# Two first feed-forward blocks built by quarters, first loads cut anew, and the joined score step's half query block read in one run

## The chip, the cores and the metric

The kernel runs on one NeuronCore of one Trainium2 chip. The metric is device time in microseconds (us) of one execution; the figure of a kernel is the median of its runs. The core's engines are TensorE (PE in the profile, with its weight loads as PEld), VectorE (DVE), ScalarE (ACT), GpSimd (POOL) and SyncE (SP). Transfers are issued by SP, ACT and POOL and carried by 16 DMA engines. POOL's transfers (queue q0) convert float32 in memory to bfloat16 on the way; those of SP and ACT (q1, q10) don't convert.

## The reference

Attention with a decay bias, then a gated feed-forward part over its output. Cut to what matters:

```python
# q, k, v: (8 batches, 8 heads, 576, 64);  s: (8, 8, 576)
scores = 0.125 * q @ k^T
cum    = cumsum(max(s, 0))
scores = where(causal, -1e9, scores + min(-(cum_i - cum_j), 0))
attn   = softmax(scores) @ v
x      = attn as (4608 tokens, 512)
xn     = x / sqrt(mean(x * x) + 1e-6) * rms_g
out    = (silu(xn @ w_gate) * (xn @ w_val)) @ w_out     # 512 -> 1536 -> 512
```

## The kernel before

**Attention.** Each batch has 4 head pairs and 5 key blocks (four of 128 rows, one of 64). K and Q of a batch are loaded, cast to bfloat16 and turned so that the head dimension lies on the partitions. A score step then has keys on the partitions and up to 256 queries (the key block's own and the next) in the free dimension; what lies further off is negligible by the decay, which a check at the end confirms, with a slow general path behind it. ACT takes the exponential, POOL masks, and the attention step multiplies with V (line 437 for the key block behind, 443 for the own one). DVE divides by the row sums, ACT or DVE sums the squares, POOL makes the scale `al_all`, DVE applies it (`x_scale`, L484), and `xs_sb` is turned into `xnT` (columns are tokens), by PE for batch 0 (`xt_step`, L504, copied out at L511).

From batch 3 on, both head groups' scores of one key block are made in one `s_run` (L339 on). Its last run of a batch joins key blocks 3 and 4: for each head pair it makes three matmuls for each half of the rows, one of 128 queries and two of the 64 tail queries (`tail`, L358), against keys 3 and keys 4. The results stand in the order r, p (query 4p + r) that the turned Q blocks have; the tail's queries stand in plain order, so `tail` is read with a step of four.

**Feed-forward.** `ffn(c)` takes 512 tokens at a time, 9 chunks. For each of 12 blocks of 128 hidden units there are four matmuls of 128x512 for the gate (`Gp`, L946), ACT's tanh (L949), four for the value (`Vp`, L955), and two DVE operations (U at L958, Ht at L951), then 4 x 12 matmuls with `wout_sb` (L972). `Gp` and `Vp` take turns in the four banks of `psF`.

**What sets the order.** The instruction order on every engine is written out by hand. Between groups of feed-forward matmuls, `step()` raises `slot[0]` by one (36 slots in a chunk) and lets at most one score step, attention step or turning step of a later batch in, by rules on slots (`can_s`, `can_av`, `can_t`); side queues (`v_side`, `pool_side`, `act_side`, `dve_side`) hold loads and casts with the slot from which they may go. Batch 0 is written out before the chunks begin: its scores, its attention, then four times `x_scale` and `do_xt`, with matmuls into nothing (`warm`, L849, and `stir`) between them. Batch 1's K and Q are loaded by SP in four transfers (`load_kq`: K heads 0 to 3, Q heads 0 to 3, K heads 4 to 7, Q heads 4 to 7) into `kq32`, cast into `kqn`, and turned in the first slots of chunk 0 (L203).

**Weights.** `load_w(src, dst, f0, f1)` lets POOL load blocks f0 to f1 (128 hidden units each, 64 KB a block as it lands) of the gate or the value matrix. Before, in POOL's order: gate 0 to 4, value 0 to 6, gate 4 to 6, and inside chunk 0 gate 6 to 12 (held back by a one-element memset of DVE in `wg_sb`, L1206), value 6 to 9 and 9 to 12, then the two tails of K and Q, V of batch 1 and `wout_sb`.

Of the kernel before, what the change touches and what calls it, by code (L numbers as in the profile page):

```python
# [26 lines left out]
def kernel(  # L27
# [12 lines left out]
    nc = tc.nc  # L40
# [298 lines left out]
    def s_run(b, kb):  # L339
# [13 lines left out]
        for g in (1, 0):  # L353
            for j in (0, 1):
                hp = 2 * g + j
                parts = [(kb, kqTx[:, p, 1, kb:kb + 2, hp, :], 0, 256)]
                if join:
                    tail = kqTx[:, p, 1, 4, hp, 0:64].rearrange("d (p r) -> d r p", r=4)  # L358
                    parts = [(3, kqTx[:, p, 1, 3, hp, :].rearrange("d (r p) -> d r p", r=4), 0, 32),
                             (3, tail, 32, 16), (4, tail, 48, 16)]  # L360
                for i, (c, qT, o, n) in enumerate(parts):
                    for par in (0, 1):
                        rs = slice(par * 64, par * 64 + 64)
                        to = banks[g][par][:, j * 256:j * 256 + 256]
                        if join:
                            to = to.rearrange("k (r p) -> k r p", r=4)[:, :, o:o + n]
                        nc.tensor.matmul(to, lhsT=keys(rs, c, hp), rhs=qT[rs],  # L367
                                         start=(j == 0 and i == 0), stop=(j == 1 and i == len(parts) - 1))
# [159 lines left out]
    K2 = 33  # L528
    slot = [0]
# [254 lines left out]
    def can_s():  # L784
# [9 lines left out]
        if b == 1 and (phase() < 24 and phase() % 2 == 0 or kb == 4 and at("AV", 1, 3, 1) > slot[0]):  # L794
            return False
# [13 lines left out]
    def can_av(clear=False):  # L809
# [5 lines left out]
        if b >= MB and last["XS"] == slot[0]:  # L815
            return False
# [119 lines left out]
    def ffn(c):  # L936

        x0 = (c * DM) % RING
        first[0], chunk[0] = slot[0], c
        Ht = mp.tile([128, FB, DM], BF16, name="Ht", tag="Ht", bufs=2)  # L940
        pend = None
        for fb in range(FB):
            fs = slice(fb * 128, (fb + 1) * 128)
            Gp = psF()
            for cc in range(CC):
                nc.tensor.matmul(Gp, lhsT=wg_sb[:, cc, fs], rhs=xnT[:, cc, x0:x0 + DM],  # L946
                                 start=(cc == 0), stop=(cc == CC - 1))
# [4 lines left out]
            step(tanh=True)  # L952
            Vp = psF()
            for cc in range(CC):
                nc.tensor.matmul(Vp, lhsT=wv_sb[:, cc, fs], rhs=xnT[:, cc, x0:x0 + DM],  # L955
                                 start=(cc == 0), stop=(cc == CC - 1))
# [4 lines left out]
            if fb < FB - 1:  # L961
                step()
# [17 lines left out]
        for tb in range(4):  # L980
            store(tb, [(0, 384), (384, 512)] if c == NCH - 1 and tb == 3 else [(0, DM)])

# [83 lines left out]
    with tc.manual_schedule():  # L1066
# [47 lines left out]

        def stir(n):
# [65 lines left out]
        for g in (0, 1):  # L1181
            for w in (0, 1):
                nc.vector.memset(kq32[0:1, w, 4 * g, 0:1], 0.0)
        for g in (0, 1):
            for w in (0, 1):
                load_kq(nc.sync, 1, w, 4 * g, 4 * g + 4)
# [22 lines left out]

# [6 lines left out]

        def load2(eng, w):
# [4 lines left out]
        def put(queue, n, *fns):  # L1222
            queue.extend((lambda: slot[0] >= n, f) for f in fns)
        put(act_side, 2, lambda: (piece1(ACT, 0, 0, 0, 4), done_cast(0, 0)))
        put(act_side, 6, lambda: piece1(ACT, 0, 1, 0, 2))
        put(pool_side, 2, lambda: fold_v(POOL, 4))
        put(pool_side, 4, lambda: (piece1(POOL, 1, 0, 0, 4), done_cast(1, 0)))
        put(pool_side, 6, lambda: (piece1(POOL, 0, 1, 2, 4), done_cast(0, 1)))
# [12 lines left out]

        check(0, (0,))
# [202 lines left out]
```

## Time and profile before

| | |
|---|---|
| median of 3 runs | 356.08 us (355.93 to 356.49) |
| the profiled execution | 355.58 us, of which the span from first to last instruction is 354.1 us |
| PE busy | 340.6 us, 96% of the span |
| DVE, ACT, POOL busy | 276.9, 213.4, 204.5 us |
| TensorE clock granted | 0.999 of full speed |
| moved by DMA | 45.68 MB, mean 129 GB/s |

Busy time of PE counts a matmul from its start to a modelled end, and matmuls overlap, so it tells less than the distance from one start to the next, which the timeline gives. A row of the timeline is: start, length, engine, line, operation, tiles, count of merged instructions, and in brackets the idle time ahead of it with what ended it. A row of the DMA view gives, for a group of transfers, the issuing queue, count, size of one, and the time from issue to landing. A row of the windows view gives busy time and count of instructions of each engine in a stretch, the granted clock, the busy share of the DMA engines (over 1 where packets overlap) and GB/s.

### The profile page before, as it was taken

What the parts mean: (1) busy time and instruction counts of PE and PEld (TensorE: products, weight loads), DVE (VectorE), ACT (ScalarE), POOL (GpSimd) and SP (SyncE); (2) the same over time, 40 slices, a digit from 0 to 9 for tenths busy, and PEclk for the clock granted to TensorE, in tenths of its full rate; (3) what the DMA queues carried; (4) which work ended last, traced back from release to release, by engine and by line L of the source; (5) the groups of instructions that cost most, each with busy time, mean ns of one, the idle gap of its engine ahead of it and who ended that gap; (6) DMA issues with size and microseconds to landing.
All of it is one profiled execution on the core that took longest, in us unless ns stands there. A gap on an engine that the chain in (4) does not pass through costs nothing.

```text
span 354.1 us, 6889 instructions
## 1 busy us (share of the span) xinstructions
PE 340.6 (96%) x2374; PEld 165.3 (47%) x2419; DVE 276.9 (78%) x524; ACT 213.4 (60%) x471; POOL 204.5 (58%) x337
## 2 busy tenths in 40 slices
PE   5989999999999999999999999999999999999995
PEld 2445444544444444444554454444544554444443
DVE  6697989598967887798889887988798659836840
ACT  3988885878786546855677557654565445224321
POOL 6969754456769986687597987597745310000000
PEclk9999999999999999999999999999999999999999
DMA  7999999999969998999899999495510121020002
GB/s 220 142 213 270 180 175 259 181 211 181 98 123 177 146 179 118 233 141 202 143 170 105 117 131 185 46 113 90 143 29 17 57 94 23 0 91 30 0 34 93
DMA packets 130528, 45.68 MB, mean 129 GB/s; under 512 B 110548, under 2 KB 125656, under 8 KB 130488
## 3 DMA queue, kind: packets, MB, share of 16 engines
q0 software_dynamic: 67056, 13.70, 50.5%
q1 hardware_dynamic: 53792, 24.20, 33.3%
q10 hardware_dynamic: 9640, 7.29, 8.2%
q8 instruction: 20, 0.33, 0.4%
q14 instruction: 20, 0.16, 0.2%
HBM read 37.90 MB, written 9.44 MB: 134 GB/s over the span
## 4 chain that ended last, share of the span: by engine, by line
PE 77%; DVE 8%; POOL 4%; issue 4%; DMA 3%; ACT 2%; SPq 0%; DVEq 0%; POOLq 0%; ACTq 0%
PE psF L972 25%; PE psF L955 21%; PE psF L946 20%; DVE U L958 2%; PE psAV L443 2%; DMA kq<-in_q_dram 2%; DMA kqT<-kqn 2%; PE psS L286 2%; DVE Ht L951 1%; PE psAV L437 1%; DVE x_sb L453 1%; PE psF L367 1%; POOL v_sb L409 1%; POOL v_sb L194 1%; PE psS L367 1%
## 5 line engine op out<-in xcount | busy, mean ns | idle before, releaser
L955 PE MATMUL psF<-xnT,wv_sb 128*128 128x512 bf16 x424 | 109.9, 379 | 0.4
L946 PE MATMUL psF<-xnT,wg_sb 128*128 128x512 bf16 x414 | 109.0, 379 | 1.3 <-ACT xnT L511 0.3
L949 ACT ACTIVATE T<-psF 128x512 f32<-128x512 f32 x108 | 64.6, 598 | 62.9 <-PE psF L946 58.8
L972 PE MATMUL psF<-wout_sb,Ht 128*128 128x512 bf16 (+2 forms) x428 | 98.9, 373 | 1.4 <-issue 0.8
L958 DVE SCALAR_TENSOR_TENSOR U<-T,psF 128x512 bf16<-128x512 f32 x108 | 73.7, 682 | 24.1 <-ACT T L949 23.9
L951 DVE TENSOR_TENSOR Ht<-U,psF 128x512 bf16<-128x512 bf16 x99 | 67.8, 685 | 6.9
L972 PEld LDWEIGHTS <-Ht 128*128 128x128 bf16 x444 | 40.1, 98 | 43.5 <-issue 1.4
L955 PEld LDWEIGHTS <-wv_sb 128*128 128x128 bf16 x432 | 39.6, 98 | 44.5 <-issue 2.9
L946 PEld LDWEIGHTS <-wg_sb 128*128 128x128 bf16 x432 | 39.4, 98 | 42.9 <-issue 2.4
L976 ACT ACTIVATE osb<-psF 128x512 f32<-128x512 f32 (+2 forms) x37 | 21.7, 587 | 58.4 <-PE psF L972 50.8
L384 POOL TENSOR_SCALAR_AFFINE_SELECT E<-E 128x512 bf16<-128x512 bf16 (+1 forms) x50 | 34.8, 704 | 28.5 <-ACT E L380 18.7
L194 POOL DMA_DIRECT2D v_sb<-in_v_dram x40 | 35.3, 885 | 0.2 <-issue 0.2
L484 DVE SCALAR_TENSOR_TENSOR xs_sb<-x_sb,al_all,g_row 128x512 bf16<-128x512 bf16 (+1 forms) x36 | 29.6, 823 | 4.1 <-POOL al_all L477 3.9
L474 POOL TENSOR_SCALAR al_all<-ss_all 128x1 f32<-128x1 f32 (+2 forms) x39 | 11.5, 295 | 35.9 <-ACT xs_sb L461 27.9
L310 ACT ACTIVATE E<-psS,biasK 128x256 bf16<-128x256 f32 (+3 forms) x88 | 29.2, 426 | 2.6 <-PE psS L286 2.6
L453 DVE TENSOR_TENSOR x_sb<-psAV,rZ 128x256 bf16<-128x256 f32 (+1 forms) x66 | 28.0, 424 | 2.3
L522 DVE TENSOR_TENSOR acc<-acc,mag 128x1280 bf16<-128x1280 bf16 x32 | 27.3, 873 | 0.2
L477 POOL TENSOR_TENSOR al_all<-al_all,mhalf 128x1 f32<-128x1 f32 (+2 forms) x39 | 25.2, 645 | 3.2
L443 PEld LDWEIGHTS <-E 128*128 128x128 bf16 x320 | 21.7, 97 | 10.5 <-POOL E L384 0.7
L461 ACT ACTIVATE xs_sb<-x_sb 128x512 bf16<-128x512 bf16 (+1 forms) x37 | 23.3, 629 | 4.6 <-DVE x_sb L453 4.0
L409 POOL TENSOR_TENSOR v_sb<-v_sb,vwx 128x512 bf16<-128x512 bf16 x25 | 25.9, 1037 | 0.1
L443 PE MATMUL psAV<-v_sb,E 128*128 128x65 bf16 x264 | 23.8, 193 | 0.1
(136 smaller groups left out, 379.8 us busy)
## 6 DMA issues: line engine op xcount, KB each, us to landing
out_dram<-osb SPq DMA_DIRECT2D x35, 256.0 KB, 2.7
kq<-in_q_dram ACTq DMA_DIRECT2D x5, 1024.0 KB, 7.5
v_sb<-in_v_dram POOLq DMA_DIRECT2D x32, 128.0 KB, 4.9
kqn<-in_k_dram POOLq DMA_DIRECT2D x20, 128.0 KB, 5.1
kq<-in_k_dram SPq DMA_DIRECT2D x4, 512.0 KB, 5.8
kq<-in_q_dram SPq DMA_DIRECT2D x4, 512.0 KB, 7.5
wout_sb<-in_moe_w_out_dram POOLq DMA_DIRECT2D x2, 768.0 KB, 10.5
kq<-in_q_dram POOLq DMA_DIRECT2D x1, 1024.0 KB, 11.0
```

The source lines that it names most:

```text
L194: nc.gpsimd.dma_start(out=v_sb[0:n, b % 2, c, :, 0:64], in_=v[b, :, c * 128:c * 128 + n, :].rearrange("h p d -> p h d"))
L384: nc.gpsimd.affine_select(out=Ev, in_=Ev, pattern=[[0, 4], [1, nq]], compare_op=ALU.is_ge, fill=0.0, base=0, channel_multiplier=-1)
L409: nc.gpsimd.tensor_tensor(out=v_sb[:, b % 2, c, :, 0:64], in0=v_sb[:, b % 2, c, :, 0:64], in1=vwx[:, c, i:i + H].unsqueeze(2).to_broadcast ...
L443: nc.tensor.matmul(o, lhsT=d, rhs=v_sb[:, p, qb, h, :], start=(j == 0 and qb == 0), stop=(j == 3))
L453: nc.vector.tensor_tensor(out=xo[:, g * 256:(g + 1) * 256].rearrange("p (h d) -> p h d", h=4), in0=pv[R, :, 0:64], in1=rZ[R].unsqueeze(2). ...
L484: nc.vector.scalar_tensor_tensor(out=xs_sb[R, (b * NSC + qb) % NX, :], in0=x_sb[R, (b * NSC + qb) % NX, :], scalar=al_all[R, col:col + 1], ...
L946: nc.tensor.matmul(Gp, lhsT=wg_sb[:, cc, fs], rhs=xnT[:, cc, x0:x0 + DM], start=(cc == 0), stop=(cc == CC - 1))
L949: nc.scalar.activation(out=T, in_=Gp, func=AF.Tanh, scale=0.5)
L951: nc.vector.tensor_tensor(out=Ht[:, fb - 1, :], in0=pend[0], in1=pend[1], op=ALU.mult)
L955: nc.tensor.matmul(Vp, lhsT=wv_sb[:, cc, fs], rhs=xnT[:, cc, x0:x0 + DM], start=(cc == 0), stop=(cc == CC - 1))
L958: nc.vector.scalar_tensor_tensor(out=U, in0=T, scalar=1.0, in1=Gp, op0=ALU.add, op1=ALU.mult)
L972: nc.tensor.matmul(Op[:, p0:p1], lhsT=Ht[:, fb, tb * 128:(tb + 1) * 128], rhs=wout_sb[:, fb, p0:p1], start=(fb == 0), stop=(fb == FB - 1))
```

## The change

There are four edits.

1. **Quarters.** Two blocks (`EARLY = 2`) of chunk 0 get their four `psF` banks before the chunk begins. `quarter(qb, i0, i1)` adds the 128 tokens of query block qb to banks i0 to i1 (gate 0, value 0, gate 1, value 1) in four matmuls of 128 columns each. Quarters 0 and 1 stand between the turning steps of x, in place of three of the four `warm(2)`; quarters 2 and 3 stand at the head of `ffn(0)`. The turning steps of x use the banks of `psAV` and `psT` in place of `psF`, and so do the turning steps of batch 1's second head pair. `ffn(0)` calls `step()` no more inside these two blocks and twice after them, and slots are counted from 2, so each later slot lies where it lay.
2. **Loads.** Value 0 to 6 is cut into 0 to 2 and 2 to 6, the second behind the first `alpha`; gate 4 to 6 becomes 4 to 8, value 6 to 12 follows it in one transfer, gate 8 to 12 goes in the first slot with an odd number from 3 on, and the memset that held POOL back is gone. K and Q heads 0 to 3 of batch 1 are loaded after the first attention step of query block 1 rather than after query block 2. The tails and V of batch 1 go two slots later.
3. **Other engines.** DVE takes one of the five products of V with its weights (`fold_v`) and the cast of K heads 0 to 3 of batch 1 (from ACT), ahead of the first U; POOL's last `fold_v` and its cast of Q heads 0 to 3 go before the chunk; two large DVE operations (`check_max`) move from before the chunk to slot 5.
4. **Joined score step.** `tail` is read in one run of 64, and the result is written with query p outside and r inside, so neighbours in the read lie 64 float32 values apart in the bank.

From the turning step of batch 1's second pair of K heads on (in the timeline of before, from 38 us), all engines have the same order as before; only the form of the tail matmuls differs.

POOL's order from batch 0's first scale to the first load inside the chunk, with the loads' sizes (128x4x512 is four blocks of a matrix) and the casts into `kqn`. Before, between the second scale and the first mask of chunk 0:

```order
L474 TENSOR_SCALAR al_all<-ss_all 128x2
L477 TENSOR_TENSOR al_all<-al_all,mhalf 128x2
L474 TENSOR_SCALAR al_all<-ss_all 128x1
L477 TENSOR_TENSOR al_all<-al_all,mhalf 128x1
L985 DMA wg_sb<-in_moe_w_gate_dram 128x4x256
L985 DMA wg_sb<-in_moe_w_gate_dram 128x4x768
L417 TENSOR_TENSOR v_sb<-v_sb,vw 128x520
L985 DMA wv_sb<-in_moe_w_val_dram 128x4x384 x2
```

The same stretch in the changed kernel (its lines are numbered a little differently):

```order
L1011 DMA wv_sb<-in_moe_w_val_dram 128x4x512
L476 TENSOR_SCALAR al_all<-ss_all 128x2
L479 TENSOR_TENSOR al_all<-al_all,mhalf 128x2
L476 TENSOR_SCALAR al_all<-ss_all 128x1
L479 TENSOR_TENSOR al_all<-al_all,mhalf 128x1
L1011 DMA wg_sb<-in_moe_w_gate_dram 128x4x512
L1011 DMA wv_sb<-in_moe_w_val_dram 128x4x768
L153 CAST kqn<-kq_75 128x256 x4
```

A load of four value blocks has come ahead of the second scale, the next gate load is four blocks where it was two, and the cast that waits for Q heads 0 to 3 stands before the last gate load.

DVE's order where batch 0's x is scaled (`xs_sb`) and the first U of chunk 0 is made. Before:

```order
L453 TENSOR_TENSOR x_sb<-psT_410,rZ 128x256
L484 SCALAR_TENSOR_TENSOR xs_sb<-x_sb,al_all,psS 128x512 x4
L516 TENSOR_SCALAR mag<-kqn 128x2560
L522 TENSOR_TENSOR acc<-acc,mag 128x1280
L1206 MEMSET wg_sb 1x1
```

and in the changed kernel:

```order
L455 TENSOR_TENSOR x_sb<-psT_412,rZ 128x256
L486 SCALAR_TENSOR_TENSOR xs_sb<-x_sb,al_all,psS 128x512 x4
L153 CAST kqn<-kq_75 128x256 x4
L518 TENSOR_SCALAR mag<-kqn 128x2560
L972 SCALAR_TENSOR_TENSOR U<-T,psF 128x512
```

Four casts of K stand where the memset and the two `acc` operations stood; before, the second `acc` and then the first U followed the memset.

The diff, cut to its core:

```diff
@@ s_run
                 if join:
-                    tail = kqTx[:, p, 1, 4, hp, 0:64].rearrange("d (p r) -> d r p", r=4)
+
+                    tail = kqTx[:, p, 1, 4, hp, 0:64]
...
                         if join:
-                            to = to.rearrange("k (r p) -> k r p", r=4)[:, :, o:o + n]
+                            to = to.rearrange("k (r p) -> k r p" if i == 0 else "k (r p) -> k p r", r=4)
+                            to = to[:, :, o:o + n] if i == 0 else to[:, o:o + n, :]
@@ do_t
                 if hp % 2:
-                    kw["pT"] = psF16()
+                    kw["pT"] = psAV16() if hp == 1 else psF16()
@@ can_s, can_av
-        if b == 1 and (phase() < 24 and phase() % 2 == 0 or kb == 4 and at("AV", 1, 3, 1) > slot[0]):
+        if b == 1 and (phase() < 24 and phase() % 2 == 0 or kb == 1 and slot[0] < 13 or kb == 4 and at("AV", 1, 3, 1) > slot[0]):
...
+        if (b, qb, g) == (1, 0, 0) and slot[0] < 16:
+            return False
@@ ffn
-        first[0], chunk[0] = slot[0], c
+        first[0], chunk[0] = (slot[0] if c else 0), c
...
+            begun = c == 0 and fb < EARLY
+            if begun:
+                Gp, Vp = early_bank[2 * fb:2 * fb + 2]
+                for i in (2 * fb, 2 * fb + 1):
+                    quarter(2, i, i + 1)
+                    quarter(3, i, i + 1)
+            else:
...
-            if fb < FB - 1:
+            if begun:
+                if fb == EARLY - 1:
+                    for _ in range(EARLY):
+                        step()
+            elif fb < FB - 1:
                 step()
...
+    def quarter(qb, i0, i1):
+        for i in range(i0, i1):
+            ws, fs = (wg_sb, wv_sb)[i % 2], slice(i // 2 * 128, i // 2 * 128 + 128)
+            for cc in range(CC):
+                nc.tensor.matmul(early_bank[i][:, qb * 128:qb * 128 + 128], lhsT=ws[:, cc, fs],
+                                 rhs=xnT[:, cc, qb * 128:qb * 128 + 128],
+                                 start=(qb == 0 and cc == 0), stop=(qb == 3 and cc == CC - 1))
...
+        def load1(g):
+
+            for w in (0, 1):
+                nc.vector.memset(kq32[0:1, w, 4 * g, 0:1], 0.0)
+            for w in (0, 1):
+                load_kq(nc.sync, 1, w, 4 * g, 4 * g + 4)
...
-        load_w(moe_w_val, wv_sb, 0, 6)
-        for c in (1, 2, 3):
+        load_w(moe_w_val, wv_sb, 0, 2)
+        for c in (2, 3, 4):
             fold_v(POOL, c)
...
         tail_step(0, psAV16())
+        fold_v(DVE, 1)
...
         do_av((0, 1, 0))
+        load1(0)
...
         alpha(0, 1)
+        load_w(moe_w_val, wv_sb, 2, 6)
...
-        load_w(moe_w_gate, wg_sb, 4, 6)
+        load_w(moe_w_gate, wg_sb, 4, 8)
+        load_w(moe_w_val, wv_sb, 6, 12)
         warm(4)
         for qb in range(4):
             x_scale(0, qb, gq)
-            do_xt((0, qb), psF16())
-            warm(2)
+        do_xt((0, 0), psAV16())
+        warm(2)
+        do_xt((0, 1), psT())
+
+        for i in range(2 * EARLY):
+            early_bank.append(psF())
+        quarter(0, 0, 2)
+        do_xt((0, 2), psAV16())
+        quarter(0, 2, 4)
+        quarter(1, 0, 1)
+        do_xt((0, 3), psT())
+        quarter(1, 1, 4)
         nc.scalar.activation(out=g_row, in_=gq, func=AF.Copy)
-        check_mag(0, 1)
-        check_max(0)
-        nc.vector.memset(wg_sb[0:1, 0, DF // 2:DF // 2 + 1], 0.0)
-        check_max(1)
-        done["check", 0, 1] = 0
...
+        piece1(POOL, 1, 0, 0, 4)
+        done_cast(1, 0)
+        piece1(DVE, 0, 0, 0, 4)
+        done_cast(0, 0)
+        check_mag(0, 1)
+        put(dve_side, 5, lambda: check_max(0), lambda: (check_max(1), done.__setitem__(("check", 0, 1), slot[0])))
...
-        put(v_side, 1, lambda: load_w(moe_w_gate, wg_sb, 6, 12))
-        put(v_side, 3, lambda: (load_w(moe_w_val, wv_sb, 6, 9), load_w(moe_w_val, wv_sb, 9, 12)))
-        put(v_side, 5, lambda: (load_tail(0), load_tail(1)))
-        put(v_side, 7, lambda: (load_v(1, 0), load_v(1, 1)))
+        put(v_side, 3, lambda: load_w(moe_w_gate, wg_sb, 8, 12))
+        put(v_side, 7, lambda: (load_tail(0), load_tail(1)))
+        put(v_side, 9, lambda: (load_v(1, 0), load_v(1, 1)))
...
+        slot[0] = 2 * EARLY - 2
         check(0, (0,))
```

More of the change, by code (lines that the diff above doesn't have):

```diff
@@ L528 @@
     K2 = 33
+    EARLY = 2
+    early_bank = []
     slot = [0]
@@ L943, in ffn @@
             fs = slice(fb * 128, (fb + 1) * 128)
[L944 to L947, printed above, removed]
+            begun = c == 0 and fb < EARLY
[5 more added lines that the diff above has]
+            else:
+                Gp = psF()
+                for cc in range(CC):
+                    nc.tensor.matmul(Gp, lhsT=wg_sb[:, cc, fs], rhs=xnT[:, cc, x0:x0 + DM],
+                                     start=(cc == 0), stop=(cc == CC - 1))
             T = mp.tile([128, DM], FP32, name="T", tag="T", bufs=2)
@@ L951, in ffn @@
                 nc.vector.tensor_tensor(out=Ht[:, fb - 1, :], in0=pend[0], in1=pend[1], op=ALU.mult)
[L952 to L956, printed above, removed]
+            if not begun:
+                step(tanh=True)
+                Vp = psF()
+                for cc in range(CC):
+                    nc.tensor.matmul(Vp, lhsT=wv_sb[:, cc, fs], rhs=xnT[:, cc, x0:x0 + DM],
+                                     start=(cc == 0), stop=(cc == CC - 1))
             U = mp.tile([128, DM], BF16, name="U", tag="U", bufs=2)
@@ L1180 @@
         norms += [do_av((0, 2, 1), psT32(), act=True, apart=True)]
[L1181 to L1186, printed above, removed]
+        load1(1)
         norms[2](False)
@@ L1220, in load2 @@
             done["raw", 2, w] = slot[0]
-        def put(queue, n, *fns):
-            queue.extend((lambda: slot[0] >= n, f) for f in fns)
-        put(act_side, 2, lambda: (piece1(ACT, 0, 0, 0, 4), done_cast(0, 0)))
         put(act_side, 6, lambda: piece1(ACT, 0, 1, 0, 2))
-        put(pool_side, 2, lambda: fold_v(POOL, 4))
-        put(pool_side, 4, lambda: (piece1(POOL, 1, 0, 0, 4), done_cast(1, 0)))
-        put(pool_side, 6, lambda: (piece1(POOL, 0, 1, 2, 4), done_cast(0, 1)))
+        put(pool_side, 5, lambda: piece1(POOL, 0, 1, 2, 4))
+        put(pool_side, 7, lambda: done_cast(0, 1))
         put(act_side, 9, lambda: piece1(ACT, 1, 1, 0, 2))
```

3 lines of the change are left out of this document (added).

## The prediction

> **What bounds the kernel now.** I read the page first, then the waits of PE, then the timeline around the first feed-forward matmul.
>
> ```profile
> PE 340.6 (96%) x2374; PEld 165.3 (47%) x2419; DVE 276.9 (78%) x524; ACT 213.4 (60%) x471; POOL 204.5 (58%) x337
> PE 77%; DVE 8%; POOL 4%; issue 4%; DMA 3%; ACT 2%; SPq 0%; DVEq 0%; POOLq 0%; ACTq 0%
> PE psF L504 <- DVE xs_sb L484: 0.5, 1, 0.5
> ```
>
> PE is busy for 96% of the span, and the chain that ended last lies on it for 77%. Its waits are short, and those that can be cut, as the 0.5 us for the first scaled x, lie ahead of the first feed-forward matmul. There PE is filled with matmuls into nothing (L849) between the turning steps (L504):
>
> ```profile
> 24.04 0.40 PE L504 MATMUL psF<-ident_bf,xs_sb 128*128 128x128 bf16 x4
> 24.27 0.59 PE L849 MATMUL psF<-mneg,ident_bf 128*128 128x512 bf16 x2
> 26.44 1.02 PE L946 MATMUL psF<-xnT,wg_sb 128*128 128x512 bf16 x4 [0.25 <-ACT xnT L511]
> 27.30 1.03 PE L955 MATMUL psF<-xnT,wv_sb 128*128 128x512 bf16 x4
> 30.22 0.39 PE L203 MATMUL psT<-ident_bf,kqn 128*128 128x128 bf16 x4
> 35.08 1.03 PE L946 MATMUL psF<-xnT,wg_sb 128*128 128x512 bf16 x4
> ```
>
> Real work begins at 26.44. Everything behind stands in one queue on PE, so a microsecond won here reaches the end unless a transfer or another engine is late for the earlier time. The DMA engines are full in just these microseconds:
>
> ```profile
> 16.60:21.00 4.40, 3.85 (x63) 2.30 (x64) 3.05 (x13) 4.40 (x12) 4.21 (x6) 1.00 0.91 129
> 21.00:24.40 3.40, 2.82 (x34) 1.74 (x32) 3.33 (x12) 2.14 (x7) 1.83 (x6) 1.00 1.15 203
> 24.40:28.40 4.00, 3.75 (x25) 1.66 (x23) 3.48 (x7) 3.18 (x7) 1.85 (x3) 1.00 1.09 350
> 29.00:31.00 2.00, 2.00 (x19) 1.10 (x20) 1.65 (x3) 1.73 (x6) 2.00 (x4) 1.00 1.24 259
> ...
> q0 software_dynamic: 64, 0.08, 11.2%
> ...
> q1 hardware_dynamic: 350, 0.35, 62.9%
> q0 software_dynamic: 333, 0.17, 61.4%
> ```
>
> The last two figures are the DMA engines' share and GB/s: never idle, 129 to 203 GB/s for POOL's converting loads alone, 350 for K and Q nearly alone, 259 for both. The queue rows (packets, MB, share) are q0's of the third stretch, the end of a weight load, and both queues' of the fourth (K and Q on q1, weights on q0), where they move about as many packets.
>
> **The quarters, if every load is there.** Two gate-and-value blocks are 16 matmuls of 512; four of them take 0.86 us (26.44 to 27.30), together 3.44. As 64 matmuls of 128 columns they cost what turning steps cost, four in 0.23 (24.04 to 24.27), together 3.7.
>
> ```profile
> 22.54 2.76 DVE L484 SCALAR_TENSOR_TENSOR xs_sb<-x_sb,al_all,psS 128x512 bf16<-128x512 bf16 x4
> 23.77 2.62 ACT L511 ACTIVATE xnT<-psF 128x512 bf16<-128x512 bf16 x4 [0.39 <-PE psF L504]
> ```
>
> DVE scales one block of x each 0.7 us, and ACT copies the first out by about 24.4. From there PE has 32 quarter matmuls (1.84) and two turning steps (0.46) to do, to 26.7, when the last copy is there; then 32 more (1.84), to 28.5, and the small score step of batch 0 (0.3 in the old place). So batch 1's first turning step stands at 28.8 instead of 30.22: **1.4 us earlier**. DVE's added `fold_v` (the nearest row of that size, U, has 0.69 us) goes into 1.36 us of waiting:
>
> ```profile
> 21.55 0.39 SPq L137 DMA_DIRECT2D kq<-in_k_dram  x1
> 18.83 0.42 DVE L453 TENSOR_TENSOR x_sb<-psAV,rZ 128x256 bf16<-128x256 f32 x1
> 17.22 0.18 DVE L451 RECIPROCAL rZ<-psAV 128x4 f32<-128x4 f32 x1 [1.36 <-PE psAV L443]
> 10.50 1.58 DVE L153 CAST kqn<-kq 128x256 bf16<-128x256 f32 x4
> 25.22 0.82 DVE L516 TENSOR_SCALAR mag<-kqn 128x2560 uint16<-128x2560 uint16 x1
> 28.13 0.69 DVE L958 SCALAR_TENSOR_TENSOR U<-T,psF 128x512 bf16<-128x512 f32 x1 [0.49 <-ACT T L949]
> ```
>
> The four casts (1.58) from the end of scaling at 25.3 and `mag` (0.82) end at 27.7, about when ACT's first tanh can be done (gate 0 is complete at 26.7 + 0.5); the two `acc` operations leave this place. Were K late, U and with it the bank of the third gate block would be late one for one, but K is issued behind the product of 18.83, at some 19.3 instead of 21.55. All this I cost at nothing, as I do POOL's moved `fold_v`, the shifted memsets and the tails' later slot.
>
> **The loads take part of it back.** The fifth gate block (35.08) now needs gate 4 to 8.
>
> ```profile
> 16.26 0.80 POOL L985 DMA_DIRECT2D wv_sb<-in_moe_w_val_dram  x1
> wv_sb<-in_moe_w_val_dram POOLq DMA_DIRECT2D x1, 768.0 KB, 9.7
> 24.24 0.84 POOL L985 DMA_DIRECT2D wg_sb<-in_moe_w_gate_dram  x1
> wg_sb<-in_moe_w_gate_dram POOLq DMA_DIRECT2D x1, 256.0 KB, 8.2
> 34.54 1.79 POOL L194 DMA_DIRECT2D v_sb<-in_v_dram  x2
> v_sb<-in_v_dram POOLq DMA_DIRECT2D x2, 128.0 KB, 8.8
> 44.48 0.29 PE L443 MATMUL psAV<-v_sb,E 128*128 128x65 bf16 x4
> ```
>
> Before, gate 4 to 6 landed at 24.24 + 8.2 = 32.4, 2.6 us ahead of use. The new order puts the same bytes ahead of this load's end and two blocks more (0.26 MB): 1.3 us at 203 GB/s or 2.0 at 129, so 33.7 to 34.4. PE wants it at 35.08 - 1.4 - 0.2 (one turning step goes behind) = 33.4. I take the middle, a wait of 0.7 (bounds 0.3 and 1.0). Value 2 to 6 is wanted near 30.3 and lies four blocks ahead of it in POOL's queue; value 0 to 2 is wanted at 24.6; value 0 to 6 landed at 16.26 + 9.7 = 26.0, and four blocks fewer (0.52 MB at 203 GB/s) make that 23.4. The second wall is V of batch 1: it landed at 43.3 and is used at 44.48, so more than 1.1 us can't be kept, as the bytes ahead of it are the same. **Kept: 0.7 us**, bounds 0.3 below nothing and 1.1.
>
> [...]
>
> **The joined step.** The three matmuls of a head pair take the same 256 columns as an unjoined one:
>
> ```profile
> 131.54 0.23 PE L367 MATMUL psF<-kqT 64*128 64x128 bf16 x1
> 131.60 0.22 PE L367 MATMUL psF<-kqT 64*128 64x64 bf16 x1
> 131.70 0.23 PE L367 MATMUL psF<-kqT 64*128 64x128 bf16 x1
> 131.87 0.53 PE L367 MATMUL psS<-kqT 64*128 64x128 bf16 x12
> 107.06 0.28 PE L367 MATMUL psF<-kqT 64*128 64x256 bf16 x1
> 107.18 0.27 PE L367 MATMUL psF<-kqT 64*128 64x256 bf16 x1
> L367 PE MATMUL psF<-kqT 64*128 64x64 bf16 x20 | 2.4, 224 | 0.1
> 29.12 0.29 PE L286 MATMUL psS<-kqT 64*128 64x64 bf16 x8
> L286 PE MATMUL psS<-kqT 64*128 64x64 bf16 x24 | 0.9, 192 | 0.0
> ```
>
> Joined, a head pair takes 0.165 us (131.54 to 131.87 for two), unjoined 0.11 to 0.12. Short matmuls with a weight load each aren't the reason: eight of 64 columns, read in one run, lie 0.03 a pair apart ((0.29 - 0.19) / 3). So a tail of 64 takes about 0.055 where 0.03 would do, and the step of four in its read is the difference that I see. With 20 in `psF`, four a run, there are 5 joined runs of 4 head pairs: 20 x 0.05 = 1.0 us, all on PE beside L972. The write that scatters has no row. Bounds: free, 1.0 won; as slow as the strided read, nothing; a quarter of full speed, 0.05 more for each of 40 tails, 2.0 lost. It's nearest to the contiguous row in all but the write, and I take **1.0**.
>
> [...]
>
> **Sum.** 0.7 + 1.0 = 1.7 us off the profiled execution's 355.6 (a span of 354.1 and 1.5 around it): 353.9. That execution lay 0.5 under the median of its runs, 356.1, so a median of **354.4**.
>
> **Rivals.** (a) The scattered write costs what the strided read cost: 356.1 - 0.7 = 355.4. For it: PE's write is as new as the read was; against it: nothing in a row. (b) The loads are in time, as the queues share sooner: 356.1 - 1.1 - 1.0 = 354.0. For it 1.24 of DMA share from 29 to 31, more overlap than either alone; against it the late start of the load at 24.24. (c) Slower: the scattered write runs at a quarter of full speed, 0.11 for a tail: 356.1 - 0.7 + 2.0 = 357.4. It decides from 0.09 a tail on, where 40 x 0.035 eats the 0.7 and as much again. For it, 40 tails stand on the engine that bounds; against it, the write of old also jumped every 16 values without a cost that I can tell from the read's. (d) The change doesn't do what it says at the start: gate 4 to 8 lands at 35 or later, since K and Q and converting loads now compete all through, PE waits 1.4 to 1.8 there, and with no gain in the joined step the median is 356.1 to 356.5.
>
> **Chances.** The forecast (0.7 and 1.0, 353.8 to 354.9) 0.38; (a) 0.24; (b) 0.15; (c) 0.13; (d) 0.10. A measurement tells 0.2% (0.7 us) from no change: below 355.4 is faster, above 356.8 slower. The forecast, (b) and nearly half of (a) are faster, 0.63; the rest of (a) and most of (d) the same, 0.20; (c) and the end of (d) slower, 0.17. The range goes from 353.2 (both terms at their upper bounds and some for a shorter start) to 357.2 (most of (c)); the likeliest case's own is 353.8 to 354.9.
>
> **What would show it.** PE's first quarter matmul at 24.4 to 24.6, the first L203 at 28.8; a PE wait for a DMA of `wg_sb` of 0.3 to 1.0 near 33.4, none for `wv_sb`; batch 1's first attention step (L443) near 43.8; head pairs of joined runs 0.11 to 0.12 apart. Wrong would be: no wait and 1.1 or more kept by 40 us (b); joined head pairs at 0.165 or more (a, c); a gate wait over 1.4, or U waiting on K's casts with PE behind it (d).

## The result and the profile after

The changed kernel takes **358.78 us** (median of 15 runs, 356.39 to 362.77) where the kernel before takes 356.47 in the same session (15 runs, 355.58 to 357.91). The ratio is 1.0071, with a 95% interval of 1.0054 to 1.0088: slower, where 354.4 was forecast, and above the whole range of 353.2 to 357.2. Runs in a slow state are left out of every ratio: here the one of 362.77, later one of 398.11 (`all_three`) and two of the kernel before (906 and 1245). The other 14 runs spread over 5.3 us, where those of before spread over 2.3. The profiled execution has 357.98.

First the page of the changed kernel (span; busy time of PE; the chain of waits by engine; the queue row of the instruction transfers: packets, MB, share), and then its waits of PE (what waited, for what, us in total, times, longest):

```profile
span 356.5 us, 7020 instructions
...
PE 342.8 (96%) x2461; PEld 166.8 (47%) x2461; DVE 278.7 (78%) x528; ACT 212.0 (59%) x467; POOL 204.4 (57%) x336
...
q8 instruction: 20, 0.33, 0.4%
...
PE 78%; DMA 7%; DVE 4%; POOL 4%; issue 3%; ACT 2%; SPq 1%; DVEq 0%; POOLq 0%; ACTq 0%
```

```profile
PE psF L369 <- DMA kqT<-kqn: 1.4, 2, 1.3
PE psF L969 <- DMA wv_sb<-in_moe_w_val_dram: 1.4, 1, 1.4
...
PE psF L959 <- DVE U L972: 0.3, 1, 0.3
```

DMA has grown from 3% to 7% of the chain. The two waits of 1.4 us for a DMA are new: one for value weights (`wv_sb`, L969) at the start, and one that nobody had thought of, at a joined score step (L369), for the DMAs that turn K and Q (`kqT` from `kqn`).

The start, in the changed kernel's timeline of PE (start, us, line and operation; in brackets the idle time that the profile sees ahead of it):

```profile
24.62 0.38 PE L1005 MATMUL psF<-xnT,wg_sb 128*128 128x128 bf16 x4
...
28.96 0.40 PE L203 MATMUL psT<-ident_bf,kqn 128*128 128x128 bf16 x4
...
30.38 0.38 PE L203 MATMUL psT<-ident_bf,kqn 128*128 128x128 bf16 x4
32.21 1.04 PE L969 MATMUL psF<-xnT,wv_sb 128*128 128x512 bf16 x4 [1.45 <-DMA wv_sb<-in_moe_w_val_dram]
...
35.24 0.19 PE L445 MATMUL psAV<-v_sb,E 128*128 128x65 bf16 x1
35.69 1.04 PE L959 MATMUL psF<-xnT,wg_sb 128*128 128x512 bf16 x4 [0.26 <-DVE U L972]
```

The quarters begin at 24.62 and batch 1's first turning step is at 28.96, 1.26 us ahead of the 30.22 of before. Then the third value block waits: it stands at 32.21 and four turning matmuls, 0.22, began at 30.38, so 1.6 us are lost; 0.4 more go ahead of the fifth gate block (35.24 to 35.69). There the profile names a U, which ended at 35.69, but the block's weights had landed only at 35.65. From 41 us on, every score step stands 0.84 us behind its place in the kernel before.

That stays so up to 168 us. There is the other loss, in the same timeline:

```profile
168.62 0.23 PE L369 MATMUL psF<-kqT 64*128 64x128 bf16 x1
...
170.11 0.21 PE L369 MATMUL psF<-kqT 64*128 64x64 bf16 x1 [1.25 <-DMA kqT<-kqn]
...
170.53 0.23 PE L369 MATMUL psF<-kqT 64*128 64x64 bf16 x1 [0.20 <-DMA kqT<-kqn]
```

From its first matmul to the start of its last, this joined run takes 2.40 us; the other four of this kernel take 0.60. In the kernel before it took 0.89 here and 0.63 elsewhere. After it the changed kernel is 2.34 behind.

The joined step itself, undisturbed, at 132 us:

```profile
132.38 0.23 PE L369 MATMUL psF<-kqT 64*128 64x128 bf16 x1
...
132.45 0.22 PE L369 MATMUL psF<-kqT 64*128 64x64 bf16 x1
...
132.48 0.24 PE L369 MATMUL psF<-kqT 64*128 64x64 bf16 x1
...
132.53 0.24 PE L369 MATMUL psF<-kqT 64*128 64x128 bf16 x1
...
132.70 0.53 PE L369 MATMUL psS<-kqT 64*128 64x128 bf16 x12
```

Two head pairs lie between 132.38 and 132.70: 0.16 each, nearly the 0.165 of before. Only the places within a pair have moved.

### The profile page after: what moved, and what is told of

Same layout as the page of the kernel before. It is cut to its first block, busy times and chain, and to the rows that moved or that the text cites. A ratio compares the mean times of both kernels' runs of the same rounds, so it can differ in the third digit from the quotient of the medians.

```text
span 356.5 us, 7020 instructions
## 1 busy us (share of the span) xinstructions
PE 342.8 (96%) x2461; PEld 166.8 (47%) x2461; DVE 278.7 (78%) x528; ACT 212.0 (59%) x467; POOL 204.4 (57%) x336
## 4 chain that ended last, share of the span: by engine, by line
PE 78%; DMA 7%; DVE 4%; POOL 4%; issue 3%; ACT 2%; SPq 1%; DVEq 0%; POOLq 0%; ACTq 0%
PE psF L990 26%; PE psF L969 21%; PE psF L959 21%; DMA wv_sb<-in_moe_w_val_dram 3%; DMA kq<-in_q_dram 2%; DMA kqT<-kqn 2%; PE psAV L445 2%; PE psS L286 2%; DVE U L972 2%; PE psAV L439 1%; PE psF L369 1%; DVE Ht L964 1%; PE psS L369 1%; POOL v_sb L411 1%; DVE x_sb L455 1%
## 5 line engine op out<-in xcount | busy, mean ns | idle before, releaser
L969 PE MATMUL psF<-xnT,wv_sb 128*128 128x512 bf16 x424 | 108.9, 379 | 1.4 <-DMA wv_sb<-in_moe_w_val_dram 1.4
L990 PE MATMUL psF<-wout_sb,Ht 128*128 128x512 bf16 (+2 forms) x444 | 100.9, 374 | 0.0
L969 PEld LDWEIGHTS <-wv_sb 128*128 128x128 bf16 x424 | 38.9, 98 | 45.6 <-issue 2.9
L959 PEld LDWEIGHTS <-wg_sb 128*128 128x128 bf16 x424 | 38.6, 98 | 41.9 <-issue 1.9
## 6 DMA issues: line engine op xcount, KB each, us to landing
kq<-in_k_dram SPq DMA_DIRECT2D x4, 512.0 KB, 5.8
kq<-in_q_dram SPq DMA_DIRECT2D x4, 512.0 KB, 7.6
wg_sb<-in_moe_w_gate_dram POOLq DMA_DIRECT2D x3, 512.0 KB, 11.2
```

What stands on the lines that cost most here:

```text
L990: nc.tensor.matmul(Op[:, p0:p1], lhsT=Ht[:, fb, tb * 128:(tb + 1) * 128], rhs=wout_sb[:, fb, p0:p1], start=(fb == 0), stop=(fb == FB - 1))
```

## The experiments

All ratios are to the kernel before, measured beside each group of runs.

**One part at a time.** `start_only` is the changed kernel with the two old lines of the joined step; `join_only` is the kernel before with the two new ones:

```diff
-                    tail = kqTx[:, p, 1, 4, hp, 0:64].rearrange("d (p r) -> d r p", r=4)
+                    tail = kqTx[:, p, 1, 4, hp, 0:64]
...
-                            to = to.rearrange("k (r p) -> k r p", r=4)[:, :, o:o + n]
+                            to = to.rearrange("k (r p) -> k r p" if i == 0 else "k (r p) -> k p r", r=4)
+                            to = to[:, :, o:o + n] if i == 0 else to[:, o:o + n, :]
```

> The changed kernel with the joined step as it was before: only the start differs from before. Theory 'loads': all that the change loses lies at the start, where it wins 1.26 us up to batch 1's first turning step and loses 1.6 us at the third value block (its weights land at 32.2) and 0.4 at the fifth gate block; the run should be 0.8 us slower than before where nothing else waits (1.002 to 1.003) and 0.2 us slower than the changed kernel. Rival 'join': the wait of 1.5 us at the joined run of 168 us and the wide spread of the changed kernel's times come from the new form of the joined step; then this kernel lacks both, and is at least 1 us faster than the changed one. Rival 'chance': that wait is a late transposing DMA that comes in some runs of any kernel; then it is seen here now and then too.

> The kernel before with the joined step of the changed one: only the joined runs differ from before. Theory 'loads': a joined run takes 0.777 us from its first matmul to its last's start and 0.81 before, so five runs win 0.17 us (0.9995 of before), and the start is as before, batch 1's first turning step at 30.2. Rival 'join': the new form makes joined runs wait for the transposing DMA (1.5 us near 167 us) and spreads the times; 1 to 2 us slower than before (1.003 to 1.006). Rival 'chance': such a wait is in some runs of before as well, and the medians agree within 0.5 us.

`start_only`: 358.98 us, 1.0087 (1.0053 to 1.0121). `join_only`: 355.81 us, 0.9991 (0.9977 to 1.0005), its joined runs 0.60 long instead of 0.63, and the work behind each 0.02 earlier. So the joined step wins about 0.1 us in all and has nothing to do with the spread (1.6 us here, 4.7 in `start_only`): the rival "join" falls. But "loads" falls too, as far as it went: it expected 1.002 to 1.003. `start_only` has a start that is some 1.6 us behind (its third value block waited 1.7; in the changed kernel the same loads cost 0.84, so the start's loss differs from one execution to the next), and it has the wait at the joined run as well, 1.65 us there and 0.6 more at a score step near 80 us. "Chance" is hard to hold when both kernels with the new start show the wait and neither with the old one does.

**The loads of the start.** `val_early` issues value 2 to 6 right behind value 0 to 2; `fine_cuts` cuts the loads in the order of use:

```diff
-        load_w(moe_w_val, wv_sb, 2, 6)
+        load_w(moe_w_val, wv_sb, 2, 4)
...
-        load_w(moe_w_gate, wg_sb, 4, 8)
-        load_w(moe_w_val, wv_sb, 6, 12)
+        load_w(moe_w_gate, wg_sb, 4, 6)
+        load_w(moe_w_val, wv_sb, 4, 6)
...
-        put(v_side, 3, lambda: load_w(moe_w_gate, wg_sb, 8, 12))
+        put(v_side, 3, lambda: (load_w(moe_w_gate, wg_sb, 6, 12), load_w(moe_w_val, wv_sb, 6, 12)))
```

> The changed kernel with value blocks 2 to 6 loaded right behind value blocks 0 to 2, 5 us earlier in POOL's order. Theory 'loads': their weights land near 27 and the third value block waits no more; K and Q of batch 1 share the engines with them and land 1 to 2 us later, so batch 1's first turning step comes at 29.5 to 30.5 instead of 28.96; the fifth gate block still waits for gate blocks 4 to 8, landing near 35, 1 us or more. Together 0 to 1 us off before. Rival: the third value block is held by its bank or by the tanh and U in front of it, then it starts near 32.2 as in the changed kernel whenever the weights land.

> The changed kernel with its weight loads cut in the order of use: value 2 to 4 in the place of 2 to 6, then gate 4 to 6 and value 4 to 6 in the place of gate 4 to 8 and value 6 to 12, and gate 6 to 12 and value 6 to 12 where gate 8 to 12 was issued. Theory 'loads': bytes ahead of each use decide; value 2 to 4 lands by 30.5 (wait under 0.4), gate 4 to 6 by 33.5 (wait under 0.5), the first turning step stays at 28.9, and 0.5 to 1.2 us are won on before in place of 0.85 lost (ratio 0.996 to 0.999). Rival: what delays such a load is the stretch before its first packet, behind K and Q, not its size; then value 2 to 4 lands at 31.5 or later, 1 us is still lost there, and the run stays at or above the time of before.

`val_early`: 359.12 us, 1.008 (1.005 to 1.0111). The value weights land at 27.8 and the third value block no longer waits, so its bank was not what held it. But K and Q of batch 1 pay: Q's first half lands at 29.4 instead of 26.8, its second at 39.1 instead of 35.5, and a turning step waits 2.0 us for its copy; this profiled execution, 360.92, is the slowest of its six. `fine_cuts`: 358.62 us, 1.0081 (1.0049 to 1.0112). Both waits of the changed kernel's start are gone, and the late one is the seventh value block, whose load I had moved behind a larger gate load (6 to 12 instead of 8 to 12). Timeline of PE in `fine_cuts`:

```profile
30.37 0.38 PE L203 MATMUL psT<-ident_bf,kqn 128*128 128x128 bf16 x4
30.59 0.81 PE L969 MATMUL psF<-xnT,wv_sb 128*128 128x512 bf16 x3
...
41.54 1.04 PE L969 MATMUL psF<-xnT,wv_sb 128*128 128x512 bf16 x4 [1.52 <-DMA wv_sb<-in_moe_w_val_dram]
```

Its start ends 0.32 us behind before, half a microsecond better than the changed kernel, and still it is at 1.008: again 0.64 us are lost at a score step near 80 us and 1.16 at 168, and this profiled execution, 357.35, is the fastest of its six. The expectation, 0.996 to 0.999, failed: the weight loads are not the whole of it.

**PE's program as a load.** What do all kernels with the new start share? 64 small matmuls take the place of 16 and of six warm-up ones: 42 matmuls more, each with its weight load (2461 loads on the page where before has 2419), 84 instructions. On an instruction queue (q8) the trace of either kernel has 20 packets of 16 KB, one for some 250 of PE's matmuls and weight loads (2 x 2461 / 20), each 0.9 to 1.8 us long. The stream that is 84 instructions longer meets them earlier in the program: the tenth begins at 165.93 us where before has it at 169.75. The DMA view of the stretch that ends where the joined run begins, before and after (queue, packets, MB, share; then issues with us to landing):

```profile
q1 hardware_dynamic: 1589, 0.38, 94.5%
q10 hardware_dynamic: 672, 0.27, 39.5%
q0 software_dynamic: 76, 0.01, 4.0%
q14 instruction: 1, 0.01, 1.0%
...
kqT<-kqn SPq DMA_TRANSPOSE x1, 5.6
```

```profile
q1 hardware_dynamic: 700, 0.17, 81.5%
q10 hardware_dynamic: 421, 0.41, 38.9%
q0 software_dynamic: 432, 0.05, 21.5%
q8 instruction: 1, 0.02, 2.7%
...
kqT<-kqn SPq DMA_TRANSPOSE x2, 6.8
```

Before (164.5 to 167.8 us) there is no packet of 16 KB: its start is at 169.75, behind the run's first matmul at 167.80. After (164.5 to 168.6) it is there, on q8 from 165.93 and 1.77 long; the packets of q1 take 81% of the engines' time though they are fewer than half as many, and the same DMA of K lands 6.8 us after its issue instead of 5.6. Two kernels test this, with nothing changed but the number of PE instructions in warm-up matmuls whose results nobody uses: 512 columns in eight pieces of 64 take the same columns.

```diff
-                nc.tensor.matmul(ps, lhsT=ident_bf, rhs=mneg, start=True, stop=True)
+                k = 8 if i < split else 1
+                for c in range(k):
+                    cs = slice(c * 512 // k, (c + 1) * 512 // k)
+                    nc.tensor.matmul(ps[:, cs], lhsT=ident_bf, rhs=mneg[:, cs], start=True, stop=True)
```

> The kernel before with 84 more instructions on PE and nothing else: six of the seven wide warm-up matmuls before 9 us (512 columns, results unused) are cut into eight of 64 columns each, which take the same columns; 84 is by how many instructions the changed kernel's PE stream is longer. Theory 'fetch': PE's program comes in packets of 16 KB on an instruction queue, one for about 250 instructions, each 0.9 to 2.0 us on one DMA engine; the longer stream moves them about 5 us earlier in the program, and the one that lay at 169.8, behind the last transposes for the joined run of 168 us, now falls on them at about 165: that run waits 0.8 to 1.5 us, the median is 1 to 3 us up (1.003 to 1.008) and the times spread. Theory 'loads' (all loss from the start's weight loads and what they shift): same as before, 0.999 to 1.001, and no wait at 168.

> The changed kernel with 168 more instructions on PE, wide warm-up matmuls before 25 us cut into eight each, so that its stream is 252 longer than before's, about one whole packet of 16 KB. Theory 'fetch': the packets lie again at the places in the program where they lay before, none on the transposes ahead of the joined run at 168; that wait is gone, the loss is what the start loses, 0.7 to 1.0 us (1.002 to 1.003), and the spread is before's. Theory 'loads': 1.006 to 1.010 as the changed kernel.

`pad_before`: 358.18 us, **1.0063** (1.0046 to 1.008). `pad_after`: 356.85 us, **1.0022** (1.0003 to 1.0042). The kernel before, given 84 instructions that do no work, loses nearly all that the change loses; the changed kernel, given 168 more, gets two thirds of its loss back. Timeline of PE in `pad_before`, where packets of 16 KB now begin at 75.74 and 166.78:

```profile
83.43 0.40 PE L286 MATMUL psS<-kqT 64*128 64x256 bf16 x4 [0.80 <-DMA kqT<-kqn]
...
168.86 0.23 PE L367 MATMUL psF<-kqT 64*128 64x128 bf16 x1
...
169.78 0.21 PE L367 MATMUL psF<-kqT 64*128 64x64 bf16 x1 [0.69 <-DMA kqT<-kqn]
...
170.72 0.21 PE L367 MATMUL psF<-kqT 64*128 64x64 bf16 x1 [0.72 <-DMA kqT<-kqn]
```

It is the same wait at the same place as in the changed kernel, and at 83 us the one of `start_only` and `fine_cuts`: this execution falls 0.87 us further behind before there and 1.48 at the joined run. One part of the expectations failed, for both kernels: the spread doesn't go with the packets. It is 1.8 us in `pad_before`, which has the waits, and 4.3 in `pad_after`, which has lost them but keeps the changed kernel's loads. The control is the kernel before with a whole packet more:

> The kernel before with 252 more instructions on PE (21 wide warm-up matmuls before 26 us cut into six more pieces each on the mean), about one packet of 16 KB. Theory 'fetch': the packets lie again where they lay in the program before, and the time is before's, 0.999 to 1.002, though more is added than in the kernel with 84, which was at 1.0063. Rival: longer streams or short warm-up matmuls cost by themselves, then this one is at 1.006 or more.

`pad_full`: 356.31 us, 0.9999 (0.9982 to 1.0015). Three times as much was added (18 warm-up matmuls in eight pieces each), and nothing was lost in the median. So it isn't the number of instructions or the short matmuls, but where the packets fall. Every one of these packets has 16 KB, and 252 instructions more bring one packet more, 21 instead of 20. All profiled executions side by side (wait: length of the joined run at 168 us over the shortest of the same kernel):

| kernel | PE instructions over before | packet of 16 KB begins | joined run begins | its wait | ratio |
|---|---|---|---|---|---|
| before | 0 | 169.75 | 167.80 | 0.26 | 1 |
| join_only | 0 | 169.57 | 168.29 | 0.12 | 0.9991 |
| join_cont | 0 | 168.94 | 167.82 | 0.06 | 0.9982 |
| join_forms (below) | 0 | 170.67 | 168.29 | about 0.6 | one run |
| changed | 84 | 165.93 | 168.62 | 1.80 | 1.0071 |
| start_only | 84 | 167.93 | 169.98 | 1.65 | 1.0087 |
| val_early | 84 | 169.25 | 171.99 | 1.45 | 1.0080 |
| fine_cuts | 84 | 166.20 | 168.74 | 1.16 | 1.0081 |
| pad_before | 84 | 166.78 | 168.86 | 1.74 | 1.0063 |
| pad_after | 252 | 172.78 | 170.37 | 0.32 | 1.0022 |
| finer_pad | 252 | 170.30 | 169.09 | 0.18 | 0.9999 |
| all_three | 252 | 169.97 | 168.68 | 0.15 | 0.9968 |
| pad_full | 252 | 171.80 | 168.72 | 1.26 | 0.9999 |

With the packet in the 2 to 3 us ahead of the run, all five waited 1.16 us or more; with it behind the run's begin, six of eight waited 0.32 or less. `pad_full` and `join_forms` are the exceptions: the profiled execution of the first (357.55, the second slowest of 12) and the only one of the second waited without such a packet. (`join_forms` has a form of the joined step there that it has nowhere else; its wait is taken over 0.63.) So the place is tight in every kernel, and the packet makes the wait the rule.

The traces also show one packet by itself, where only the queue of the turning DMAs is busy beside it. The DMA that turns K, issued at 253.15 us in the kernel before and at 256.07 in `pad_before` (DMA view of about a microsecond from its issue on):

```profile
q8 instruction: 1, 0.02, 8.1%
...
kqT<-kqn SPq DMA_TRANSPOSE x1, 3.6
```

```profile
kqT<-kqn SPq DMA_TRANSPOSE x1, 2.3
```

In all eight kernels with 0 or 252 instructions more, a packet begins while this DMA is under way, and it takes 3.5 to 4.1 us; in the five with 84 none does, and it takes 2.3. For the K issued at 247.60 in the kernel before it is the other way round: 4.0 to 4.3 in the five, which have the packet there, and 2.7 in the eight. So in these two places such a DMA is longer by 1.2 us or more with a packet under way. In fuller stretches the difference can vanish (the x issued at 148.89: 5.9 to 7.1 with, 5.6 to 7.0 without), but near 74 us, ahead of the score step at 83, the DMA that turns x takes 7.2 to 8.0 us in the five, with the packet under way, and 5.4 to 6.4 in the eight.

**A start that loses nothing.** `finer_pad` is `fine_cuts` with the 168 added instructions and gate and value loads 6 to 9 and 9 to 12 in turn.

> As the run before it (168 more instructions), and the weight loads are cut finely in the order of use: value 2 to 4, gate 4 to 6, value 4 to 6, gate 6 to 9, value 6 to 9, gate 9 to 12, value 9 to 12. Theory 'fetch' with 'loads': no wait at the third value block (30.6), at the fifth gate block (33.6) or at the seventh value block, where the coarse cut waited 1.5 us; the first turning step at 28.95 is kept up to the wall that V of batch 1 sets (landing near 43.4 for a use near 43.3), so 0.5 to 1.2 us are won by 50 us, and the run ends at 0.996 to 0.999 of before. Rival: what these loads win comes back as a wait at V of batch 1 or at W out, 1 us or more, and the run is not faster than before.

It takes 356.13 us, 0.9999 (0.9987 to 1.0011): the rival. The weights are there in time (0.4 us ahead of before at 43 us), and V of batch 1, behind all these loads, lands at 45.3 and is late; x of chunk 1 costs 0.47 more near 68 us. Its timeline of PE:

```profile
43.84 0.39 PE L506 MATMUL psT<-ident_bf,xs_sb 128*128 128x128 bf16 x4
45.31 0.29 PE L445 MATMUL psAV<-v_sb,E 128*128 128x65 bf16 x4 [1.09 <-DMA v_sb<-in_v_dram]
```

**The joined step's pattern.** `join_forms` is the kernel before with another form in each of the five batches that have a joined step.

> The kernel before, with another form of the joined step's reads and writes in each of the five batches that have one (scores of these batches land in other places, so the output is not the reference's): first all reads and writes contiguous; second the tail read by steps of four; third the tail written in runs of 16; fourth the tail written with a jump at each element; fifth the old write of all parts with a contiguous read. In all but the fifth block 3 is written contiguously. Theory 'pattern': each step of four in a read and each jumping write halves the speed of a tail: from a joined run's first matmul to its last's start the first and the fifth take 0.50 to 0.58, the second and the fourth 0.75 to 0.82 us. Theory 'weights': three loads of two weight tiles for each head pair set the time, whatever the pattern; all five take 0.75 to 0.82.

Timeline of PE: the first form (all contiguous), the fourth (a jump at each element written) and the fifth (old write, contiguous read):

```profile
132.26 0.23 PE L380 MATMUL psF<-kqT 64*128 64x128 bf16 x1
...
132.38 0.22 PE L380 MATMUL psF<-kqT 64*128 64x128 bf16 x1
...
132.50 0.28 PE L380 MATMUL psS<-kqT 64*128 64x128 bf16 x6
...
241.31 0.23 PE L380 MATMUL psF<-kqT 64*128 64x128 bf16 x1
...
241.46 0.24 PE L380 MATMUL psF<-kqT 64*128 64x128 bf16 x1
...
241.63 0.25 PE L380 MATMUL psS<-kqT 64*128 64x128 bf16 x2
...
277.41 0.23 PE L380 MATMUL psF<-kqT 64*128 64x128 bf16 x1
...
277.54 0.22 PE L380 MATMUL psF<-kqT 64*128 64x128 bf16 x1
...
277.65 0.22 PE L380 MATMUL psS<-kqT 64*128 64x128 bf16 x2
```

Two head pairs take 0.24, 0.32 and 0.24 us. From its first matmul to its last's start a run takes 0.44 in the first, the third (writes in runs of 16) and the fifth form, and 0.60 in the fourth; the second (strided read) waited for its DMA, and where it ran freely a head pair took 0.17 to 0.18. My absolute figures were 0.06 to 0.22 too long, the order is that of "pattern", and "weights" falls, since six weight loads a head pair fit into 0.11. A tail read by steps of four and a tail written with a jump at each element cost nearly the same (0.63 and 0.60 a run in the kernels before and after); a write in runs of 16 costs nothing.

**The step without either.** `join_cont` is the kernel before with contiguous reads and writes, and ACT brings the order about:

```diff
-                to = to.rearrange("k j (p r) -> k j p r", r=4)
-                src = src.rearrange("k (j r p) -> k j p r", j=2, r=4)
+                src = src.rearrange("k (j n) -> k j n", j=2)
+                nc.scalar.activation(out=to[:, :, 128:256], in_=src[:, :, 128:256], func=AF.Exp, scale=0.125)
+                to = to[:, :, 0:128].rearrange("k j (p r) -> k j p r", r=4)
+                src = src[:, :, 0:128].rearrange("k j (r p) -> k j p r", r=4)
```

`all_three` joins it to `finer_pad` and puts V of batch 1 and the tails ahead of gate and value 9 to 12.

> The kernel before with the joined step all contiguous: block 3 and both tails are read and written in one run each, and ACT's exponential, which puts the scores into order, is two instructions for a score tile of a joined step instead of one (20 more in all). By the forms measured before, a head pair takes 0.11 instead of 0.167 us and a joined run 0.79 instead of 1.02 to the next work: 5 x 0.23 = 1.15 us won, 0.997 of before. Rival: ACT's longer exponentials (two of 256 elements for one of 512) hold back the attention steps or the bank's next use; then PE waits for ACT near 132, 168, 205, 241 and 277 us, and it is 0.998 or more.

> The finely cut loads with the 168 added instructions, as measured before at 0.9999, and two things more: V of batch 1 and the tails are loaded ahead of gate and value 9 to 12 (V landed at 45.3 for a use at 43.95, gate 9 to 12 at 40.9 for a use at 48.0), and the joined step is all contiguous as in the run beside it. Theory: the wait of 1.1 us for V goes and the joined step wins 1.1: 0.993 to 0.996 of before. Rival: another transfer takes V's place as the wall (gate 9 to 12, the tails, W out), then only the joined step's part is won, 0.997.

`join_cont`: 355.43 us, 0.9982 (0.9964 to 1.0001). In its trace each joined run is shorter by 0.19 and the work behind it comes 0.23 earlier, 1.1 us in all, without a wait for ACT; this execution is the fastest of its twelve, the median shows 0.7 of it, and the interval just touches 1. `all_three`: 355.26 us, **0.9968** (0.995 to 0.9986), faster than both kernels. V of batch 1 is used at 44.20 without a wait. But the rival holds in its profiled execution, since another transfer takes V's place: its start keeps 0.28 us, 1.37 are lost at the first gate block of chunk 1, and the joined runs win 1.24 of it back. Its timeline of PE:

```profile
68.34 0.39 PE L959 MATMUL psF<-xnT,wg_sb 128*128 128x512 bf16 x1 [1.19 <-DMA xnT<-xs_sb]
```

In the kernel before, that DMA landed 0.6 us ahead of its use.

## Why the prediction was wrong

**The quarters: right.** First quarter matmul at 24.62 (24.4 to 24.6 forecast), first turning step of batch 1 at 28.96 (28.8), 1.26 us won (1.4). The work of other engines that I costed at nothing stayed hidden up to there.

**The loads: the term was mis-sized, and its first half wrong.** The prediction let 0.7 us go at the fifth gate block and had value 2 to 6 in time, since it "lies four blocks ahead of it in POOL's queue" and four blocks fewer had landed at 23.4. That second figure was right (value 0 to 2 landed at 23.7), but it says nothing about value 2 to 6, whose issue had moved from 16.3 to 21.3 and so to behind the first halves of K and Q. The DMA view of the changed kernel from 15 to 34 us, with its POOL timeline:

```profile
21.32 0.84 POOL L1011 DMA_DIRECT2D wv_sb<-in_moe_w_val_dram  x1
24.44 0.81 POOL L1011 DMA_DIRECT2D wg_sb<-in_moe_w_gate_dram  x1
```

```profile
wg_sb<-in_moe_w_gate_dram POOLq DMA_DIRECT2D x3, 512.0 KB, 11.2
...
wv_sb<-in_moe_w_val_dram POOLq DMA_DIRECT2D x1, 512.0 KB, 10.8
```

Value 2 to 6 landed at 21.32 + 10.8 = 32.1 and gate 4 to 8 at 24.44 + 11.2 = 35.6, not at 33.7 to 34.4. (A block is 128 KB as it lands, as the 512.0 KB of four show, not the 64 KB given with the kernel before; the sums had the right bytes.) The rows of before had 8.2 us from issue to landing for two blocks and 9.7 for six. Laid on the issue at 21.3 they give 29.5 to 31.0, on both sides of the use at 30.3, so a wait there belonged among the terms; I laid such a duration on the gate load alone. In the profiled execution the start wins 1.26 and then loses 2.1: it ends 0.84 us behind and does not win 0.7. Rival (b), by which the queues share sooner and the loads are in time, falls as well: issued at 21.32 with K and Q under way, this load took 10.8 us.

**The joined step: rival (a).** About 0.1 us won, not 1.0. The strided read was the cost of the old step, as argued; the scattered write, "nearest to the contiguous row in all but the write", costs as much. A joined run with the scattered write takes 0.60 us, against 0.44 all contiguous (`join_forms`); a head pair with the read by steps of four takes 0.17, against 0.11.

**What no step had: PE's own program.** The prediction gives 64 small matmuls only the time that they take on PE. These and their weight loads made the stream 84 instructions longer, and so moved the packets of 16 KB to other places (the tenth from 169.75 to 165.93 us). In the profiled execution 1.5 us go at the joined run of 168 us. In the medians, `pad_after`, whose packets are back in their places, is 0.7 us slower than before (356.85 against 356.16); the rest, 1.6 of the 2.3 us, goes with the packets, and `pad_before` shows them alone, 2.0 us. That the start's 0.84 and the joined step's 0.1 also add up to 0.7 is partly luck: with the same loads the start of `start_only` lost 1.6 us and that of `pad_after` 2.6 in their profiled executions.

**What stays open.** The runs show that the packets' places decide, that the wait ends with the turning DMAs, and that such a DMA is longer with a packet under way at three places (near 74, 248 and 253 us; at the last 3.6 us in the kernel before against 2.3 in `pad_before`). By what way one packet holds a DMA up they don't show. Nor do they show why the start's loss differs so much between executions; the wide spread goes with the changed loads (5.3, 4.7 and 4.3 us in the three kernels that have them as changed), and its cause was not tested.

## What to carry to other kernels

Here 84 instructions more on an engine that is busy for 96% of the span moved its program's own transfers along the program (165.93 us instead of 169.75) and, doing no work, cost 2.0 us in `pad_before`. Where a change loses time far from what it touches, and the waits there are for DMAs with little margin, add as many idle instructions to the kernel before and see whether the loss comes too, and add a whole packet's worth (here 252: 0.9999) to see it go. When loads are recut, lay the whole time from issue to landing on each load whose issue moves, and look for the next wall behind it (here value 2 to 6, gate 4 to 8, value 6 to 12, V of batch 1, x of chunk 1, one after the other). Here a permutation cost TensorE nearly the same in the read and in the write (0.63 and 0.60 us a run against 0.44), so give it to an engine that isn't the bound, or keep runs of 16 in the write.

## What the hardware showed unexpectedly

PE's program came in packets of 16 KB, one for about 250 matmuls and weight loads, 0.9 to 1.8 us each in the traces before and after; 84 idle instructions cost 2.0 us in the median and 252 nothing. Near 253 us a DMA that turns K took 3.5 to 4.1 us with such a packet under way and 2.3 without; for one that turns x near 149 us there was hardly a difference (5.9 to 7.1 against 5.6 to 7.0). Matmuls of 64 columns took about twice their time when the columns were read with a step of four bfloat16 (8 bytes) or written with a jump at each element of 256 or 128 bytes, and no longer than contiguous ones when written in runs of 16 elements (0.44 us a run in both): a head pair with two such tails took 0.17 or 0.16 us instead of 0.11, of which a contiguous tail has 0.03. Eight warm-up matmuls of 64 columns in place of one of 512 took no time that could be seen: the first turning step moved by 0.1 us in `pad_before`.
